# Casting the two halves of P around the relu in an attention and FFN kernel, with one VectorE order changed behind a hash

## The chip, the cores and the metric

The kernel runs on one core of a Trainium2 chip. The metric is the device time of one execution in microseconds; the kernel before took 977.11 us (median of three runs, 977.09 to 977.16).

A core has engines that work side by side, each through its own list of instructions in order: TensorE (PE; its weight loads are shown apart as PEld), VectorE (DVE), ScalarE (ACT), GpSimd (POOL) and SyncE (SP), which here issues nearly all DMAs.

## The reference

Attention with a hash mask over 32 heads (4 batches of 8, 768 tokens, 64 dimensions), and an FFN over its 3072 tokens:

```python
q_bits = (np.einsum('bhsd,dk->bhsk', q, proj) > 0).astype(np.int64)
k_bits = (np.einsum('bhsd,dk->bhsk', k, proj) > 0).astype(np.int64)
q_bucket = np.sum(q_bits * powers, axis=-1)
k_bucket = np.sum(k_bits * powers, axis=-1)
mask = q_bucket[:, :, :, None] == k_bucket[:, :, None, :]
scores = np.where(mask, scale * np.matmul(q, k.transpose(0, 1, 3, 2)), -1000000000.0)
attn = np.exp(scores - np.max(scores, axis=-1, keepdims=True))
attn = attn / (np.sum(attn, axis=-1, keepdims=True) + 1e-09)
x = np.matmul(attn, v)            # heads side by side: 3072 x 512
h = x @ w_in                      # 512 x 2048
g = h * np.clip(h + 3.0, 0.0, 6.0) / 6.0
return (g @ w_out).astype(np.float32)
```

## The kernel before, in words

Every operand of a large matmul is split into a high part, rounded to the PE's faster fp32 form, and a low part, the rest. So each product is made of two or three passes, and each operand costs a cast (ACT) and a subtraction (DVE or POOL).

The work is cut into steps k, one for each head and each block of 128 queries (32 heads x 6 blocks = 192 steps). From step 102 on (`GT`) the attention of batches 2 and 3 runs beside the FFN of batches already done; this is the function `beside_ffn`, and the change lies in it. The FFN takes 256 tokens at a time (a chunk) and 16 slices of its hidden dimension (`fc`), so one slice for each step, and a chunk for 16 steps. The order of each engine's instructions is the order in which the code issues them; only SP's order is chosen by a scheduler.

One step k from 102 on issues, in this order:

- PE, odd k only: `values_whole` (L512), a block of twelve matmuls that multiplies V with P of steps k-3 and k-2: three matmuls each for the high part of half 0, the high part of half 1, the low part of half 0, the low part of half 1. A half is 384 of the 768 keys.
- DVE: `lowest` (L396), called rounding in the change's title, reads the scores of step k+2 from PSUM, caps them and finds the lowest.
- ACT and DVE: the gate's split of the FFN slice of step k-1 (`split_g`): a cast to the high part (L681), and the low part (L682).
- ACT: the exponential of step k+2 (L408). DVE: its transposition in blocks of 32 (`flip`, L429). SP: the DMA that writes it to DRAM (`fd`), from where a later step's four DMAs read it back rearranged (`move`, into `px` or `spare` in turn). A buffer is free for the next `move` when the casts and subtractions of a step have read it.
- `split_p` of step k-1, for half 0 and half 1: two casts on ACT (L475, one row x2 in the timeline), then the subtraction of half 0 on DVE (L479) and of half 1 on POOL (L477).
- PE: the first product of the FFN slice (`gemm1`, L653). ACT: in even steps, a copy of the output of the last block of L512 (L542, `y<-acc`).
- PE, one step in six: the hash products of the next head (L334 to L336).
- PE: the second product of the slice before (`gemm2`, L691, L692 with the gate's high part, L696 with its low part). ACT: the relu (L675). DVE: the gate's product (L676). When the slice before was the last of its chunk, ACT also copies the FFN's result out of PSUM (L710, two instructions). This is in the part called `go("C")`.
- DVE, where there was a hash: its bits (L352). PE: the scores of step k+3 (L387, L389). At the end of a chunk the next tokens are split (casts on ACT, L642; low parts on DVE, L643).

The gate's high and low part have one buffer, so its cast waits for the second product of the slice before.

Of the kernel before, what the change touches and what calls it, by code (L numbers as in the profile page):

```python
# [28 lines left out]
LA = 3  # L29
# [3 lines left out]
LT = 1  # L33
# [10 lines left out]
def lsh_attention_moe(  # L44
# [10 lines left out]
    nc = tc.nc  # L55
# [3 lines left out]
    KT = S // P  # L59
    HW = S // 2  # L60
    QT = HW // P
# [31 lines left out]
    def bank(shape, name: str, tag: str | None = None):  # L93

        nonlocal turn
        if tag is None:
            tag = ("pt", "pu")[turn % 2]
            turn += 1
        return ps.tile(shape, F32, name=name, tag=tag, bufs=2)
# [128 lines left out]
    NS = NJ * KT  # L228
# [3 lines left out]
    GT = GF + FT  # L232
# [37 lines left out]
    def scale_q(i: int):  # L270

        for c in spans(i):
            if paced:
                nc.scalar.mul(raws[i][:D, c], raws[i][:D, c], -SCALE)
            else:
                nc.gpsimd.tensor_scalar_mul(raws[i][:D, c], raws[i][:D, c], -SCALE)
# [114 lines left out]
    def lowest(g: int):  # L391

        s = scs.pop(g)
        m = sp.tile([P, 1], F32, name=f"m{g}", tag="m", bufs=4)
        pr_ = sp.tile([P, 2, HW], F32, name=f"p{g}", tag="p", bufs=2)
        nc.vector.tensor_scalar(  # L396
            out=pr_[:], in0=s[:, :, :HW], scalar1=CAP, scalar2=None,
            op0=ALU.min, op1=ALU.min, accum_out=m[:],
        )
        probs[g] = pr_, m  # L400
# [82 lines left out]
    def split_lows():  # L483
        for f in lows:
            f()
        lows.clear()
# [18 lines left out]
    def values_whole(u: int):  # L505
        vv = vvs[2 * u // KT]
        acc = accs[u] = bank([P, 2 * P], f"acc{u}")
        both = [parts.pop((u, c)) for c in range(2)]
        for part in range(2):
            for kt in range(KT):  # L510
                c, x = divmod(kt, QT)
                nc.tensor.matmul(  # L512
                    acc[:], lhsT=vv[:, kt], rhs=both[c][part][:, x],
                    start=(part == 0 and kt == 0), stop=(part == 1 and kt == KT - 1),
                )

    adds = []

# [263 lines left out]
    def cv(n: int):  # L782

        if n < NW:
            if n not in conv:
                conv[n] = convert(n)
            next(conv[n])
# [299 lines left out]
    with tc.manual_schedule(engines={ET.PE, ET.DVE, ET.Activation, ET.Pool}):  # L1087
        split_qk(0, None)
        hash_qk(0)
        bits(0)  # L1090
        scale_q(1)
        split_v(0)
        for x in range(3):
            ahead(0, x)
        for _ in range(2):
            cv(0)
        def go(part: str):
            if stage == part:
                next(fill, None)

        through = []

        def beside_ffn(k: int):

            nonlocal paced, stage, held
            held = False
            if k < GT:
                for c in range(2):  # L1110
                    transp(k, c)
                exponential(k + 1)
            for _ in range(2):
                u = vnext // 2
                if u < NS // 2 and (2 * u < GT or k % 2 and k >= 2 * u + 3):
                    if vnext % 2 == 0 and k >= GT:
                        value_whole()
                        through.append(u)
                        break
                    if value_half():  # L1120
                        through.append(vnext // 2 - 1)
                if k < GT:
                    break
            if k == GT:
                opening.pop()()
            if k + 2 < NS and k >= GT:
                lowest(k + 2)
            go("A")
            if k < GT:
                for c in range(2):  # L1130
                    split_p(k, c, False)
                split_lows()
                while through:
                    output(through.pop(0))
                flip(k + 1)
            if k + 2 < NS:
                if k < GT:
                    lowest(k + 2)
                exponential(k + 2)
            paced = True  # L1140
            multiply()
            if k + 2 < NS:
                flip(k + 2)
            if GT <= k - LT < NS:
                for c in range(2):
                    split_p(k - LT, c, False)
            split_lows()
            go("B")
            if k == NS + LT:
                homes.clear()  # L1150
            while through and (through[0] < vnext // 2 - 1 or k % 2 == 0 or k < GT):
                output(through.pop(0))
            hashed = k + LA < NS and (k + LA) % KT == 4 and (k + LA) // KT + 1 < NJ
            if hashed:
                hash_qk((k + LA) // KT + 1)
            go("C")
            if hashed:
                bits((k + LA) // KT + 1)
            if k + LA < NS:
                lead(k + LA)  # L1160
            if moves:
                moves.pop(0)()
            if GT <= k + 1 < NS:
                move(k + 1)

            place_in_chunk = (k - GT) % NFC
            if subs and (k % 2 and (k < GT or place_in_chunk != NFC - 1) or k > GT and place_in_chunk == 0):
                subs.pop(0)()
            go("D")
            if k % KT in (1, 3):  # L1170
                add()

        for k in range(NS + LT + 2):
            if k >= GT - 1:
                beside_ffn(k)
                continue
            end = GB if k < GB else NS
            i, t = divmod(k, KT)
            if k == HK - XE:
                lent += lents[cc3:]  # L1180
            if k == GB:
                lent.clear()
            if k == HK:
                late["x"] = sp.tile([P, S], F32, name="late", tag="raw", bufs=1)
            for c in range(2):
                transp(k, c)
            if k + 1 < end:
                exponential(k + 1)
            if k + 2 < end:
                lowest(k + 2)  # L1190
            if k == GB:
                next(first)
                pair_turn = 0

            third = True
            whole = False
            for _ in range(1 if k != HK else 2):
                if vnext < k - k % 2:
                    whole = value_half()
            held = k >= GF - 2  # L1200
            if held:
                next(fill, None)
            if whole and k >= GF:
                output(vnext // 2 - 1)
                whole = False

            hashed = k >= GF and (k + LA) % KT == 2
            if k >= GF and k + LA < end and not hashed:
                lead(k + LA)
            for c in range(2):  # L1210
                split_p(k, c, third)
            split_lows()
            multiply()
            held = False
            if (k < GF or hashed) and k + LA < end:
                if hashed:
                    if (k + LA) // KT + 1 < NJ:
                        hash_qk((k + LA) // KT + 1)
                        bits((k + LA) // KT + 1)
                    next(fill, None)  # L1220
                lead(k + LA)
            if k == GB - 2:
                hash_qk((GB - 1) // KT + 1)
                bits((GB - 1) // KT + 1)
            if whole:
                output(vnext // 2 - 1)
            if k >= GF - 2 and not hashed:
                next(fill, None)
            if k < GB:
                for f in early_steps[k]:  # L1230
                    f()

            if k < HK and t == 1 and i:
                with tc.issue_after(last.ins):
                    load_w(i)
            if k == HK:
                add()
                late_x()
                with tc.issue_after(last.ins):
                    get_qk(H + 2)  # L1240
                    for n in range(WE, WL):
                        load_w(n)
            if k + 1 == GB:
                first = first_ffn(lambda part: ahead(GB, part))
                next(first)
                for _ in range(2):
                    whole = value_half()
                output(vnext // 2 - 1)
                next(first)
        paced = False  # L1250
        assert vnext == NS and not through
        add()
        for _ in fill:
            pass
# [47 lines left out]
```

## Time and profile before

| | |
|---|---|
| median of three runs | 977.11 us |
| profiled execution | 976.93 us |
| its span | 975.2 us |
| granted TensorE clock, mean | 0.997 |
| PE, PEld, DVE, ACT, POOL busy | 98%, 90%, 74%, 64%, 49% |
| matmuls of L512, steps beside the FFN | 552 |

The span is the time from the first to the last instruction that the profile shows. A row of the timeline has the start in us, the duration, the engine, the line, the operation, what it writes and reads, and how many instructions were merged; in brackets stands how long its engine was idle before it and what ended that. A row of the waits has the total in us, how often, and the longest. In the window's row PE, PEld, DVE, ACT and POOL follow each other, then the clock, the share of DMA and GB/s. Matmuls overlap, so a merged row of PE ends later than the next one begins.

### The profile page before, as it was taken

What the parts mean: (1) busy time and instruction counts of PE and PEld (TensorE: products, weight loads), DVE (VectorE), ACT (ScalarE), POOL (GpSimd) and SP (SyncE); (2) the same over time, 40 slices, a digit from 0 to 9 for tenths busy, and PEclk for the clock granted to TensorE, in tenths of its full rate; (3) what the DMA queues carried; (4) which work ended last, traced back from release to release, by engine and by line L of the source; (5) the groups of instructions that cost most, each with busy time, mean ns of one, the idle gap of its engine ahead of it and who ended that gap; (6) DMA issues with size and microseconds to landing.
All of it is one profiled execution on the core that took longest, in us unless ns stands there. A gap on an engine that the chain in (4) does not pass through costs nothing.

```text
span 975.2 us, 19413 instructions
## 1 busy us (share of the span) xinstructions
PE 951.2 (98%) x6306; PEld 875.4 (90%) x6306; DVE 716.8 (74%) x1476; ACT 626.9 (64%) x1421; POOL 480.8 (49%) x498
## 2 busy tenths in 40 slices
PE   8999999999999998899999999999999999999997
PEld 7999888999989998799999889999999899889896
DVE  7999988888569998777777778878777774342422
ACT  6898875656478887567766666676676664333332
POOL 6777744655537775355555546546556542000000
PEclk9999999999999999999999999999999999999999
DMA  3567579100035544688798787788787772101000
GB/s 118 139 163 179 133 237 374 42 2 1 6 118 126 124 111 123 181 249 237 227 258 243 230 245 235 234 264 243 237 266 229 218 225 69 44 1 44 1 22 22
DMA packets 113116, 151.65 MB, mean 156 GB/s; under 512 B 13764, under 2 KB 82116, under 8 KB 113016
## 3 DMA queue, kind: packets, MB, share of 16 engines
q1 hardware_dynamic: 108456, 144.79, 48.7%
q0 software_dynamic: 4560, 5.64, 4.8%
q8 instruction: 50, 0.82, 0.4%
q14 instruction: 50, 0.41, 0.1%
HBM read 77.34 MB, written 53.61 MB: 134 GB/s over the span
## 4 chain that ended last, share of the span: by engine, by line
PE 80%; DVE 9%; issue 3%; POOL 3%; DMA 2%; ACT 2%; SPq 1%; DVEq 0%; ACTq 0%; POOLq 0%
PE h L653 26%; PE po L696 6%; PE po L691 6%; PE po L692 6%; PE acc L500 6%; PE acc L512 6%; PE s L389 5%; PE s L387 5%; PE pt L418 5%; DVE p L396 3%; DVE pl L479 2%; POOL pl L477 2%; DVE qq L352 1%; PE z L334 1%; PE z L335 1%
## 5 line engine op out<-in xcount | busy, mean ns | idle before, releaser
L408 ACT ACTIVATE p<-p,m 128x768 f32<-128x768 f32 x192 | 180.2, 939 | 92.7 <-DVE p L396 87.9
L396 DVE TENSOR_SCALAR_CACHE_REDUCE p<-s 128x768 f32<-128x768 f32 x192 | 182.9, 953 | 40.4 <-PE s L389 24.9
L676 DVE SCALAR_TENSOR_TENSOR h<-g,h 128x256 f32<-128x256 f32 x192 | 81.9, 426 | 95.3 <-ACT g L675 93.4
L675 ACT ACTIVATE g<-h,three 128x256 f32<-128x256 f32 x192 | 91.0, 474 | 91.5 <-PE h L653 89.6
L653 PE MATMUL h<-xh,w 128*128 128x256 f32 x1024 | 147.0, 283 | 1.6 <-ACT xh L642 1.6
L653 PEld LDWEIGHTS h<-xh,w 128*128 128x128 f32 x1024 | 135.7, 189 | 5.1 <-ACT xh L642 1.8
L429 DVE STREAM_TRANSPOSE p<-p 128x768 f32<-128x768 f32 x90 | 88.1, 979 | 60.3 <-ACT p L408 60.3
L477 POOL TENSOR_TENSOR pl<-spare,ph 128x384 fp32r<-128x384 f32 x45 | 62.4, 1388 | 117.7 <-ACT ph L475 82.2
L479 DVE TENSOR_TENSOR pl<-pt,ph 128x384 fp32r<-128x384 f32 x196 | 100.0, 550 | 3.5 <-ACT ph L475 3.0
L681 ACT CAST gb<-h 128x256 fp32r<-128x256 f32 x141 | 52.5, 372 | 77.2 <-DVE h L676 44.0
L387 PE MATMUL s<-kk,qq 76*128 76x384 f32 x384 | 100.1, 341 | 1.8 <-ACT kk L357 1.5
L389 PE MATMUL s<-kk,qq 128*128 128x384 f32 x384 | 100.4, 343 | 0.0
L692 PE MATMUL po<-w,gb 128*128 128x512 f32 x250 | 98.3, 393 | 0.0
L691 PE MATMUL po<-w,gb 128*128 128x512 f32 x250 | 98.3, 393 | 0.0
L477 POOL TENSOR_TENSOR pl<-px,ph 128x384 fp32r<-128x384 f32 x45 | 61.6, 1370 | 72.6 <-ACT ph L475 58.5
L475 ACT CAST ph<-pt 128x384 fp32r<-128x384 f32 x196 | 86.0, 473 | 14.7 <-PE pt L418 12.7
L216 POOL TENSOR_TENSOR w<-wr,w 128x128 fp32r<-128x128 f32 x128 | 72.0, 594 | 45.2 <-ACT w L210 42.1
L418 PE MATMUL pt<-ident,p 128*128 128x128 f32 x612 | 85.9, 274 | 3.6 <-DVE pl L479 2.7
L418 PEld LDWEIGHTS pt<-ident,p 128*128 128x128 f32 x612 | 71.7, 141 | 11.1 <-PE pt L418 2.5
L653 PE MATMUL h<-xl,w 128*128 128x256 f32 x512 | 81.5, 281 | 0.0
L696 PE MATMUL po<-w,gb 128*128 128x512 f32 x250 | 78.8, 396 | 1.5 <-DVE gb L682 1.5
L387 PEld LDWEIGHTS s<-kk,qq 76*128 76x128 f32 x384 | 66.7, 190 | 11.3 <-ACT kk L357 2.1
(153 smaller groups left out, 2133.4 us busy)
## 6 DMA issues: line engine op xcount, KB each, us to landing
fd<-p SPq DMA_DIRECT2D x90, 384.0 KB
spare<-fd SPq DMA_DIRECT2D x180, 96.0 KB
px<-fd SPq DMA_DIRECT2D x180, 96.0 KB
kk<-qq SPq DMA_DIRECT2D x62, 192.0 KB
wr<-in_w_in SPq DMA_DIRECT2D x16, 512.0 KB
wr<-in_w_out SPq DMA_DIRECT2D x16, 512.0 KB
raw<-in_qkT SPq DMA_DIRECT2D x19, 384.0 KB
vr<-in_v SPq DMA_DIRECT2D x32, 192.0 KB
```

The source lines that it names most:

```text
L387: nc.tensor.matmul(s[:, c, :HW], lhsT=q1[:KM, us], rhs=half(k1[:KM], c), start=True, stop=False)
L389: nc.tensor.matmul(s[:, c, :HW], lhsT=q2[:, us], rhs=half(k2, c), start=False, stop=True)
L396: nc.vector.tensor_scalar(out=pr_[:], in0=s[:, :, :HW], scalar1=CAP, scalar2=None, op0=ALU.min, op1=ALU.min, accum_out=m[:],)
L408: nc.scalar.activation(pr_[:], pr_[:], AF.Exp, bias=m[:], scale=-1.0, accum_out=sms[b][:, t, h : h + 1])
L418: nc.tensor.transpose(pt[:, x], probs[g][0][:, c, x * P : (x + 1) * P], ident[:])
L477: engine.tensor_sub(lo, pt, hi.bitcast(F32))
L479: lows.append(lambda: engine.tensor_sub(lo, pt, hi.bitcast(F32)))
L653: nc.tensor.matmul(hp, lhsT=wi[:, wp, wc], rhs=x[cc][xp], start=(k == 0 and cc == 0), stop=(k == 2 and cc == NCC - 1),)
L675: nc.scalar.activation(r[:], hp, AF.Relu, bias=three[:], scale=1.0)
L691: nc.tensor.matmul(po[u], lhsT=gh[:, us], rhs=wo[:, 0], start=(fc == 0), stop=False)
L692: nc.tensor.matmul(po[u], lhsT=gh[:, us], rhs=wo[:, 1], start=False, stop=False)
L696: nc.tensor.matmul(po[u], lhsT=gl[:, us], rhs=wo[:, 0], start=False, stop=(fc == NFC - 1))
```

## The change

In `beside_ffn`, for the steps from 102 on, half 1 of P (POOL's) is cast first, and half 0 (DVE's) only behind `go("C")`, that is, behind the relu; its subtraction stands behind the gate's product on DVE. `values_whole` takes half 1 ahead of half 0. In the step behind one with a hash, the gate's low part comes ahead of `lowest` on DVE.

```diff
         both = [parts.pop((u, c)) for c in range(2)]
+        first, end = (0, 1, 0), (1, 0, QT - 1)
         for part in range(2):
-            for kt in range(KT):
-                c, x = divmod(kt, QT)
-                nc.tensor.matmul(
-                    acc[:], lhsT=vv[:, kt], rhs=both[c][part][:, x],
-                    start=(part == 0 and kt == 0), stop=(part == 1 and kt == KT - 1),
-                )
+            for c in (1, 0):
+                for x in range(QT):
+                    nc.tensor.matmul(
+                        acc[:], lhsT=vv[:, c * QT + x], rhs=both[c][part][:, x],
+                        start=(part, c, x) == first, stop=(part, c, x) == end,
+                    )
...
-            if k + 2 < NS and k >= GT:
+            behind = (k - 1 + LA) % KT == 4
+            if GT <= k < NS - 2 and not behind:
                 lowest(k + 2)
             go("A")
+            if GT <= k < NS - 2 and behind:
+                lowest(k + 2)
...
-            if GT <= k - LT < NS:
-                for c in range(2):
-                    split_p(k - LT, c, False)
-            split_lows()
+            split = GT <= k - LT < NS
+            if split:
+                split_p(k - LT, 1, False)
             go("B")
...
             go("C")
+            if split:
+                split_p(k - LT, 0, False)
+            split_lows()
```

On ACT at step 118, where a chunk of the FFN ends (`ph` are the casts of P, `y` the copy of a block's output, `g` the relu, `ob` the copies of the FFN's result, `gb` the gate's cast), the rows before:

```order
L408 ACTIVATE p_6545,sms_5284<-p_6545,m_6544 128x768
L475 CAST ph_0_6490<-px 128x3x128
L475 CAST ph_1_6493<-px 128x3x128
L542 COPY y_0_6571<-acc_6466 128x256
L675 ACTIVATE g_1_0_6580<-h_1_0_6558,three 128x256
L710 ACTIVATE ob_0_6583<-po_0_5595 128x512 x2
L681 CAST gb_1_0_6614<-h_1_0_6558 128x256
```

And now, at the same place (line numbers have moved by one):

```order
L408 ACTIVATE p_6545,sms_5284<-p_6545,m_6544 128x768
L475 CAST ph_1_6490<-px 128x3x128
L543 COPY y_0_6569<-acc_6466 128x256
L676 ACTIVATE g_1_0_6578<-h_1_0_6556,three 128x256
L711 ACTIVATE ob_0_6581<-po_0_5595 128x512 x2
L475 CAST ph_0_6516<-px 128x3x128
L682 CAST gb_1_0_6614<-h_1_0_6556 128x256
```

The cast of half 0 has moved behind the y copy, the relu and both copies of the FFN's result; in a step inside a chunk the rows are the same without the `ob` row.

On DVE at steps 133 and 134, where a hash, the end of a chunk and the step behind the hash come together (`pl` is the low part of P's half 0, `h` the gate's product, `qq` the hash bits, `xl` the next tokens' low parts, `gb` the gate's low part, `m` marks `lowest`), the rows before:

```order
L429 STREAM_TRANSPOSE p_7470<-p_7470 128x768
L479 TENSOR_TENSOR pl_0_7481<-spare,ph_0_7480 128x3x128
L676 SCALAR_TENSOR_TENSOR h_1_15_7488<-g_1_15_7515,h_1_15_7488 128x256
L352 TENSOR_SCALAR qq_7261<-z_0_7501,thr,val 44x384
L352 TENSOR_SCALAR qq_7261<-z_1_7502,thr,val 44x384
L643 TENSOR_TENSOR xl_2_7534<-xr_2_7132,xh_2_7533 128x256 x4
L396 TENSOR_SCALAR p_7545,m_7544<-s_7524 128x768
L682 TENSOR_TENSOR gb_1_15_7547<-h_1_15_7488,gb_1_15_7547 128x256
```

And now:

```order
L429 STREAM_TRANSPOSE p_7470<-p_7470 128x768
L677 SCALAR_TENSOR_TENSOR h_1_15_7484<-g_1_15_7511,h_1_15_7484 128x256
L479 TENSOR_TENSOR pl_0_7515<-spare,ph_0_7514 128x3x128
L352 TENSOR_SCALAR qq_7261<-z_0_7497,thr,val 44x384
L352 TENSOR_SCALAR qq_7261<-z_1_7498,thr,val 44x384
L644 TENSOR_TENSOR xl_2_7534<-xr_2_7128,xh_2_7533 128x256 x4
L683 TENSOR_TENSOR gb_1_15_7544<-h_1_15_7484,gb_1_15_7544 128x256
L396 TENSOR_SCALAR p_7548,m_7547<-s_7524 128x768
```

The low part of P's half 0 has moved behind the gate's product, and the gate's low part ahead of `lowest`.

On PE the block of L512 (here of step 109) keeps its place; its halves have changed theirs. Before:

```order
L389 MATMUL s_5943<-kk_5455,qq_5456 128x384 x2
L512 MATMUL acc_5953<-ph_0_5862,vv_5662 128x256 x3
L512 MATMUL acc_5953<-ph_1_5865,vv_5662 128x256 x3
L512 MATMUL acc_5953<-pl_0_5863,vv_5662 128x256 x3
L512 MATMUL acc_5953<-pl_1_5866,vv_5662 128x256 x3
```

And now:

```order
L389 MATMUL s_5943<-kk_5455,qq_5456 128x384 x2
L513 MATMUL acc_5953<-ph_1_5862,vv_5662 128x256 x3
L513 MATMUL acc_5953<-ph_0_5888,vv_5662 128x256 x3
L513 MATMUL acc_5953<-pl_1_5863,vv_5662 128x256 x3
L513 MATMUL acc_5953<-pl_0_5889,vv_5662 128x256 x3
```

The block now begins with POOL's half, and the high part of DVE's half is read from the fourth matmul on, the low part of POOL's half from the seventh.

## The prediction

> **What bounds the kernel now.** I read the page first, then the waits and the windows of the stage that the change touches, then the chain of waits and the timeline of single steps.
>
> ```profile
> span 975.2 us, 19413 instructions
> PE 951.2 (98%) x6306; PEld 875.4 (90%) x6306; DVE 716.8 (74%) x1476; ACT 626.9 (64%) x1421; POOL 480.8 (49%) x498
> ```
> ```profile
> 396.00:820.00 424.00, 418.03 (x2698) 384.68 (x2696) 321.41 (x635) 279.55 (x653) 223.86 (x195) 1.00 0.79 234
> ```
> ```profile
> PEld acc L512 <- POOL pl L477: 5.1, 12, 0.5
> PEld po L696 <- DVE gb L682: 3.2, 4, 1.4
> PE acc L512 <- POOL pl L477: 2.7, 11, 0.3
> ```
> PE bounds the kernel. In the stage of the change (396 to 820 us: steps 102 to 190) it is idle for 424.00 - 418.03 = 6.0 us, at full clock, with DMA at 0.79. What ends last there is the low part of P that POOL makes (L477), ahead of the matmuls at L512. The chain of waits shows what a block of twelve such matmuls takes:
> ```profile
> 423.98 1.57 PE acc L512 x12
> ...
> 432.56 1.59 PE acc L512 x12
> ...
> 459.86 1.42 PE acc L512 x12
> ...
> 800.78 1.57 PE acc L512 x12
> ```
> Of the stage's 45 blocks 19 look like the first, second and fourth row; the third has other PE work ahead of it and waits for nothing. A regular block thus loses 1.57 - 1.42 = 0.15 us. One of them in full (step 108, and the block of step 109):
> ```profile
> 431.03 0.91 ACT L475 CAST ph<-px 128x384 fp32r<-128x384 f32 x2
> 431.85 0.36 ACT L542 COPY y<-acc 128x256 f32<-128x256 f32 x1
> 432.11 0.47 ACT L675 ACTIVATE g<-h,three 128x256 f32<-128x256 f32 x1
> ```
> ```profile
> 431.16 0.98 DVE L429 STREAM_TRANSPOSE p<-p 128x768 f32<-128x768 f32 x1 [0.76 <-ACT p L408]
> 432.06 0.52 DVE L479 TENSOR_TENSOR pl<-px,ph 128x384 fp32r<-128x384 f32 x1
> 432.62 0.43 DVE L676 SCALAR_TENSOR_TENSOR h<-g,h 128x256 f32<-128x256 f32 x1
> ```
> ```profile
> 432.07 1.39 POOL L477 TENSOR_TENSOR pl<-px,ph 128x384 fp32r<-128x384 f32 x1 [1.42 <-DMA spare<-fd]
> ```
> ```profile
> 432.22 0.84 PEld L512 LDWEIGHTS acc<-ph,vv 128*128 128x128 f32 x6
> 433.00 0.94 PEld L512 LDWEIGHTS acc<-pl,vv 128*128 128x128 f32 x6
> 433.87 0.43 PEld L653 LDWEIGHTS h<-xh,w 128*128 128x128 f32 x3
> ```
> The wait sits on the weight load. Loads follow each other by about 0.12 us, so the tenth (first of POOL's half) is due at 433.00 + 3 x 0.12 = 433.36; POOL ends at 433.46, a signal takes 0.05 (POOL's end at 478.54 + 1.41 = 479.95 and the load at 480.00, both below), and 0.15 are lost.
>
> **The change, part by part: regular blocks.** POOL's cast goes first: two casts take 0.91, the second begins 0.41 behind the first, so POOL can start at about 431.60 instead of 432.07. How long its subtraction takes then is shown by a step where DVE's came early:
> ```profile
> 565.50 0.56 DVE L479 TENSOR_TENSOR pl<-spare,ph 128x384 fp32r<-128x384 f32 x1 [0.27 <-ACT ph L475]
> ...
> 565.90 1.02 POOL L477 TENSOR_TENSOR pl<-spare,ph 128x384 fp32r<-128x384 f32 x1 [3.20 <-ACT ph L475]
> ```
> 1.02 alone against 1.39 beside DVE's. With 1.02 it ends at 432.62, with 1.39 at 432.99; its matmuls are now the seventh to ninth, whose first load is due at 433.00, so it must end by 432.95. I take 1.02, since DVE's subtraction now comes after it: spare 0.33. At 1.39 it would miss by 0.04. The Trainium skill ("SBUF — State Buffer", Who interferes with whom) says the same of the cause: a VectorE instruction with two SBUF inputs and a GpSimd instruction that reads SBUF share a port pair, and the later one blocks wholly; by that rule 1.02 holds wherever POOL is first. The two rows agree with the price, but at 432.06 both start together and POOL alone pays, so the order of the records does not tell who gets it.
>
> DVE's half goes later. The y copy follows the one remaining cast at 431.44, the relu 0.26 later at 431.70, and what follows a relu starts 0.37 behind it (478.62 to 478.99, below), so the cast of DVE's half runs from 432.07 to 432.57. Its matmuls are now the fourth to sixth, whose first load is due half way from 432.22 to 433.00, the span of the first six loads: at 432.61. With the signal's 0.05 it comes at 432.62, just in time. DVE's subtraction then ends at 433.12, due at 433.31. I take no wait: 19 x -0.15 = -2.85 us; bounds 0 (a cast 0.15 late) and -2.85.
>
> **Chunk ends.** Every 16 steps ACT also copies the FFN's result out (L710, 10 instructions in the stage, so five steps: 118, 134, 150, 166, 182). Step 118 and the block of step 119:
> ```profile
> 477.54 0.91 ACT L475 CAST ph<-px 128x384 fp32r<-128x384 f32 x2
> 478.35 0.37 ACT L542 COPY y<-acc 128x256 f32<-128x256 f32 x1
> 478.62 0.48 ACT L675 ACTIVATE g<-h,three 128x256 f32<-128x256 f32 x1
> 478.99 1.08 ACT L710 ACTIVATE ob<-po 128x512 f32<-128x512 f32 x2
> 479.94 0.39 ACT L681 CAST gb<-h 128x256 fp32r<-128x256 f32 x1
> ```
> ```profile
> 478.32 0.84 PEld L512 LDWEIGHTS acc<-ph,vv 128*128 128x128 f32 x6
> 479.13 0.41 PEld L512 LDWEIGHTS acc<-pl,vv 128*128 128x128 f32 x3
> 480.00 0.41 PEld L512 LDWEIGHTS acc<-pl,vv 128*128 128x128 f32 x3 [0.46 <-POOL pl L477]
> 480.35 1.01 PEld L653 LDWEIGHTS h<-xh,w 128*128 128x128 f32 x8
> ```
> ```profile
> 478.54 1.41 POOL L477 TENSOR_TENSOR pl<-px,ph 128x384 fp32r<-128x384 f32 x1 [3.65 <-ACT ph L475]
> ```
> Today both casts stand ahead of the two copies and the block loses 480.35 - 478.32 - 1.42 - 0.06 = 0.55 (0.06: loads from the block's first to the next line's span 433.87 - 432.22 = 1.65 in the regular block, which counts 1.59). Afterwards the cast of DVE's half stands behind them: one cast less ahead, so relu at 478.21, copies at 478.58 and 479.06, cast from 479.53 to 480.04. Its load is due half way from 478.32 to 479.13, at 478.73, and comes at 480.09: 1.36 late, 0.81 worse than today. Lower bound: +0.3, if such a step starts no later than a regular one; upper: +1.3.
>
> **Behind a hash** (every sixth step) the gate's low part (L682) goes ahead of the rounding (L396). Mostly the scores that the rounding waits for come after it: 0.03 lost. Not where DVE is late already, at steps 134 and 182 (a chunk end too) and 128 and 176:
> ```profile
> 547.79 1.92 DVE L643 TENSOR_TENSOR xl<-xr,xh 128x256 fp32r<-128x256 f32 x4
> 549.74 0.96 DVE L396 TENSOR_SCALAR_CACHE_REDUCE p<-s 128x768 f32<-128x768 f32 x1
> 550.63 0.08 DVE L396 DVE_READ_ACCUMULATOR p<-s 128x1 f32 x1
> 550.63 0.42 DVE L682 TENSOR_TENSOR gb<-h,gb 128x256 fp32r<-128x256 f32 x1
> ```
> ```profile
> 551.10 0.30 PEld L696 LDWEIGHTS po<-w,gb 128*128 128x128 f32 x2 [0.46 <-DVE gb L682]
> ```
> There the rounding starts 0.34 later (0.42 less the overlap of 0.08) and with it the exponential, the casts and the block. PE's wait for the low part at 551.10 goes, but the block behind it takes that back, since it waits for ACT anyway. So 0.81 + 0.34 = 1.15 at 134 and 182. At 128 and 176 the lateness grows by 0.34 and by about 0.25 that DVE loses when its subtraction, now behind the gate, waits for POOL: 0.6 each.
>
> The sum: regular -2.85; chunk ends 3 x 0.81 + 2 x 1.15 = +4.7; 128 and 176 +1.2; of the other irregular blocks seven have casts that are late for other reasons, and there the cast that now comes 0.63 later (432.07 against 431.44) costs between -0.15 and +0.4, taken as +0.2: +1.4. Together +4.5 on the profiled execution's 976.93 (span 975.2 and 1.7 around it; the median of the runs is 977.11, 0.2 more): 981.5. Other moves cost nothing: POOL, SP and PE keep their instructions, and bits and x's splits on DVE still end before the next scores.
>
> **Rivals.** *The regular cast misses too* (chance 0.20, slower): it has nothing to spare. A y copy or relu that starts 0.15 later undoes the gain of all 19: 981.5 + 2.85 = 984.4. Against it: the ACT rows are the same within 0.02 in the regular blocks.
>
> *Transfers come earlier* (0.18, no change): POOL's input buffer is free when the later subtraction ends, at 433.12 instead of 433.46, and the move into it can go 0.34 earlier. Where a step waits for transfers today,
> ```profile
> 568.28 0.96 DVE L396 TENSOR_SCALAR_CACHE_REDUCE p<-s 128x768 f32<-128x768 f32 x1 [1.63 <-PE h L653]
> ```
> ```profile
> 569.64 0.30 PEld L696 LDWEIGHTS po<-w,gb 128*128 128x128 f32 x2 [0.88 <-DVE gb L682]
> ```
> (the 1.63 of idle time end with a DMA; the PE work named was long done) PE loses 0.88 and, in the block behind it, as much as in another late one, 0.55: 1.4. Two more places wait for casts whose input lands late; at half of that each the whole is 2.8, and the time 981.5 - 2.8 = 978.7. Against it: after a chunk end the buffer is free later.
>
> *DVE catches up* (0.12, faster): the first of the four splits at 547.79 takes 0.9 instead of 0.4 behind a POOL instruction; POOL now ends 0.8 earlier in each step. If each late step caught up 0.9, chunk ends would cost 5 x (1.36 - 0.90 - 0.55) = -0.4, steps 128 and 176 nothing, the seven -1.0, and the whole -4.3: 972.7. It decides from 0.8 of relief per chunk end; the rows show 0.5.
>
> **The numbers.** The main case has 0.50. A measurement of this kernel can tell 0.2% (2 us) from no change. Faster 0.12, the same 0.18, slower 0.70. The range reaches from 978.0, below the case of transfers, to 985.5, above that of the missed cast; the faster case and the tails are left out.
>
> **What would show it.** Right: blocks of 1.42 after regular steps; POOL's subtraction at about 1.0; the load of the fourth matmul after a chunk end waiting for ACT's cast by over 1 us, five times. Wrong: regular blocks that wait for ACT's cast (the first rival), or chunk-end blocks near 2.0 us as today.

## The result, and the profile after

The changed kernel takes 986.75 us (median of four runs, 985.31 to 989.38), the kernel before 977.13 beside it (four runs, 977.09 to 977.99): a ratio of 1.0099, interval 1.0076 to 1.0123. It is slower, as forecast, but by 9.6 us where 4.4 were forecast, and above the range. The profiled execution took 985.31, 8.4 more than the 976.93 of before.

The head of the page after:

```profile
span 983.5 us, 19374 instructions
PE 952.3 (97%) x6306; PEld 875.9 (89%) x6306; DVE 727.8 (74%) x1476; ACT 626.9 (64%) x1421; POOL 456.3 (46%) x498
```

POOL works 24.5 us less and DVE 11 more. The same stretch of the stage, and two short stretches in it (the last three numbers of a row are the granted clock, the share of DMA and GB/s):

```profile
396.00:820.00 424.00, 410.87 (x2644) 378.27 (x2643) 328.24 (x625) 276.13 (x644) 198.14 (x194) 0.99 0.80 233
...
480.00:485.00 5.00, 3.99 (x21) 3.79 (x22) 3.56 (x5) 2.23 (x6) 2.11 (x2) 0.73 0.65 226
485.00:490.00 5.00, 5.00 (x29) 4.51 (x28) 3.36 (x6) 2.55 (x6) 2.24 (x2) 0.93 0.79 238
```

PE is idle for 13.1 us of the stretch instead of 6.0, and at one place its clock is low, which it never was in the stage before after 410 us. What PE waits for at the block of twelve matmuls, now L513, in the waits of the stage:

```profile
PEld acc L513 <- ACT ph L475: 11.2, 14, 1.5
PE acc L513 <- ACT ph L475: 9.4, 13, 1.3
...
PEld acc L513 <- DVE pl L479: 1.9, 3, 0.6
```

POOL's low part is gone from the list. In its place stand the cast of half 0 (ACT), and, three times, the low part of half 0 (DVE).

A regular block came out as forecast. The step 108 and the block of step 109 in the timeline after, all engines in one list:

```profile
431.50 0.50 ACT L475 CAST ph<-px 128x384 fp32r<-128x384 f32 x1
...
432.12 1.02 POOL L477 TENSOR_TENSOR pl<-px,ph 128x384 fp32r<-128x384 f32 x1 [1.37 <-ACT ph L475]
...
432.53 0.51 ACT L475 CAST ph<-px 128x384 fp32r<-128x384 f32 x1
...
432.68 0.84 PEld L513 LDWEIGHTS acc<-ph,vv 128*128 128x128 f32 x6
...
433.07 0.56 DVE L479 TENSOR_TENSOR pl<-px,ph 128x384 fp32r<-128x384 f32 x1
...
433.45 0.79 PEld L513 LDWEIGHTS acc<-pl,vv 128*128 128x128 f32 x6
```

POOL's subtraction takes 1.02 instead of 1.39, the second cast comes 1.03 behind the first and is just in time, and the loads show no wait. The chain of waits has the block of this step, and that of the regular step before it, at the length of a block without a wait:

```profile
424.59 1.43 PE acc L513 x12
433.02 1.43 PE acc L513 x12
```

The end of a chunk did not. Step 118 and the block of step 119 in the timeline after:

```profile
478.60 1.01 POOL L477 TENSOR_TENSOR pl<-px,ph 128x384 fp32r<-128x384 f32 x1 [4.26 <-DMA spare<-fd]
478.68 0.48 ACT L676 ACTIVATE g<-h,three 128x256 f32<-128x256 f32 x1
478.77 0.49 PEld L513 LDWEIGHTS acc<-ph,vv 128*128 128x128 f32 x3
...
479.05 1.08 ACT L711 ACTIVATE ob<-po 128x512 f32<-128x512 f32 x2
...
479.69 1.82 POOL L318 TENSOR_TENSOR kk<-raw,qq 64x768 fp32r<-64x768 f32 x1
480.00 0.53 ACT L475 CAST ph<-px 128x384 fp32r<-128x384 f32 x1
...
480.56 1.37 DVE L479 TENSOR_TENSOR pl<-px,ph 128x384 fp32r<-128x384 f32 x1 [0.94 <-DMA kk<-qq]
480.58 0.41 PEld L513 LDWEIGHTS acc<-ph,vv 128*128 128x128 f32 x3 [1.32 <-ACT ph L475]
...
481.98 0.43 PEld L513 LDWEIGHTS acc<-pl,vv 128*128 128x128 f32 x3 [0.63 <-DVE pl L479]
...
482.33 0.73 PEld L654 LDWEIGHTS h<-xh,w 128*128 128x128 f32 x3
```

By the prediction's measure (first load of the block to the first load of the next line, less 1.48) the block loses 482.33 - 478.77 - 1.48 = 2.08 us, 0.55 before. Two waits make it up: for the cast, which the prediction has, and for DVE's subtraction, which it has not. That one takes 1.37 instead of 0.55, because it meets L318, in which POOL splits a head's keys for the hash.

Where the next tokens' high parts stand behind the moved cast, the first product of the new chunk is late too; its load at step 118, after (before, 0.36 behind the line ahead of it as everywhere, with no wait):

```profile
474.09 0.37 PEld L389 LDWEIGHTS s<-kk,qq 128*128 128x128 f32 x2
474.75 1.57 PEld L654 LDWEIGHTS h<-xh,w 128*128 128x128 f32 x8 [0.29 <-ACT xh L643]
```

### The profile page after: what moved, and what is told of

It is laid out like the page before. It is cut to its first block, busy times and chain, and to the rows that moved or that the text cites. A ratio compares the mean times of both kernels' runs of the same rounds, so it can differ in the third digit from the quotient of the medians.

```text
span 983.5 us, 19374 instructions
## 1 busy us (share of the span) xinstructions
PE 952.3 (97%) x6306; PEld 875.9 (89%) x6306; DVE 727.8 (74%) x1476; ACT 626.9 (64%) x1421; POOL 456.3 (46%) x498
## 4 chain that ended last, share of the span: by engine, by line
PE 77%; DVE 9%; ACT 4%; DMA 3%; issue 3%; SPq 1%; POOL 1%; ACTq 0%; DVEq 0%; POOLq 0%
PE h L654 25%; PE po L697 6%; PE po L692 6%; PE po L693 6%; PE acc L500 6%; PE acc L513 5%; PE pt L418 5%; PE s L389 5%; PE s L387 5%; DVE p L396 3%; DVE pl L479 3%; ACT ph L475 2%; DVE qq L352 1%; SPq L78 1%; DMA spare<-fd 1%
## 5 line engine op out<-in xcount | busy, mean ns | idle before, releaser
L477 POOL TENSOR_TENSOR pl<-spare,ph 128x384 fp32r<-128x384 f32 x45 | 45.7, 1016 | 140.0 <-ACT ph L475 79.6
L475 ACT CAST ph<-pt 128x384 fp32r<-128x384 f32 x196 | 86.1, 473 | 15.1 <-PE pt L418 13.1
L477 POOL TENSOR_TENSOR pl<-px,ph 128x384 fp32r<-128x384 f32 x45 | 46.1, 1024 | 73.7 <-ACT ph L475 50.2
```

The costliest lines, as they stand in the source:

```text
L475: nc.scalar.copy(hi, pt)
L477: engine.tensor_sub(lo, pt, hi.bitcast(F32))
```

## The experiments

The theory behind the first of them: the loss comes from the five chunk ends, where the cast of half 0 stands behind the two copies of the FFN's result; what goes beyond the forecast there is DVE's subtraction beside POOL's L318, and a lower clock behind long waits. The rivals: the loss is spread over the steps (the exchange behind a hash, or transfers), or the order of the casts itself is wrong. The times of a run stand beside runs of the kernel before on the same chip, 976.66 to 977.06 by the median.

**The cast ahead of the copies.** In the changed kernel the cast and the subtraction of half 0 are issued ahead of the copies where a chunk ends; everywhere else they stay. (The FFN's code empties the list below just ahead of its copies.)

```diff
             if split:
-                split_p(k - LT, 0, False)
-            split_lows()
+                ahead_of_copies.append(lambda: late_half(k - LT))
+            go("C")
+            while ahead_of_copies:
+                ahead_of_copies.pop(0)()
```

> The changed kernel, with one thing different: at the five chunk ends the cast of DVE's half stands behind the relu but ahead of the two copies of the FFN's result (0.96 us of ACT). Theory (chunk ends: the cast waits behind the copies, then DVE's subtraction behind a POOL instruction, then a lower granted clock): the wait for the cast falls from 1.28 to 1.60 us to 0.3 to 0.6 at each of the five, the 0.68 behind the low part goes at three of them or stays, no stretch at a clock of 0.7; 978 to 981 us. Rival (DVE's two new orders are what costs: the subtraction behind the gate's product, the gate's low part ahead of the rounding): within 1.5 us of the changed kernel's 986.8.

It took 978.02 us (976.37 to 980.04, ten runs), a ratio of 1.0011 (0.9998 to 1.0023) to before: 8.7 of the 9.6 us are gone, with everything else of the change in place. The block of step 119 in its timeline:

```profile
479.89 0.48 PEld L513 LDWEIGHTS acc<-ph,vv 128*128 128x128 f32 x3
...
480.71 0.56 DVE L479 TENSOR_TENSOR pl<-px,ph 128x384 fp32r<-128x384 f32 x1
480.73 0.41 PEld L513 LDWEIGHTS acc<-ph,vv 128*128 128x128 f32 x3 [0.36 <-ACT ph L475]
...
480.82 2.17 POOL L318 TENSOR_TENSOR kk<-raw,qq 64x768 fp32r<-64x768 f32 x1
481.08 0.79 PEld L513 LDWEIGHTS acc<-pl,vv 128*128 128x128 f32 x6
```

The wait for the cast falls from 1.32 to 0.36, and the one for the low part is gone: DVE's subtraction now starts 0.11 ahead of L318, takes 0.56, and L318 pays (2.17 instead of 1.82). In the stretches from 410 us on no clock is below 0.98. So the chunk ends hold the loss; which of the three parts has how much is for the next two runs.

**POOL's subtraction of the keys one step later.** In the changed kernel, at two of the five chunk ends (steps 118 and 166), L318 moves to the step behind.

```diff
+            hold = k > GT and place_in_chunk == 0 and k % KT == 4
-            if subs and (k % 2 and (k < GT or place_in_chunk != NFC - 1) or k > GT and place_in_chunk == 0):
+            if subs and (k % 2 and (k < GT or place_in_chunk != NFC - 1) or k > GT and place_in_chunk == 0 and not hold):
+                subs.pop(0)()
+            if subs and k > GT and place_in_chunk == 1 and k % KT == 5:
                 subs.pop(0)()
```

> The changed kernel with POOL's 1.82 us subtraction of a head's keys moved one step on, at two of the five chunk ends (steps 118 and 166). Theory (VectorE's subtraction takes 1.37 instead of 0.55 us there only because POOL's subtraction of the keys runs beside it): the waits of 0.69 us for the low part go at blocks 119 and 167 and stay at 151, the time is 984 to 985.5 (986.75 less 1.36, and less up to 1.5 where the low clock behind block 119 goes too), unless the two subtractions that POOL then has in the step behind make a wait of their own. Rival (the low part is late by its place in VectorE's order, whatever POOL does): the waits of 0.69 stay and the time is 986.75.

It took 985.04 us (983.41 to 986.51, five runs). In its timeline DVE's subtraction at step 118, and then the step behind with the two moved subtractions:

```profile
480.57 0.56 DVE L479 TENSOR_TENSOR pl<-px,ph 128x384 fp32r<-128x384 f32 x1 [0.94 <-DMA kk<-qq]
...
484.64 2.03 POOL L318 TENSOR_TENSOR kk<-raw,qq 64x768 fp32r<-64x768 f32 x1
...
486.75 1.84 POOL L318 TENSOR_TENSOR qq<-raw,qq 64x768 fp32r<-64x768 f32 x1
...
488.67 1.01 POOL L477 TENSOR_TENSOR pl<-px,ph 128x384 fp32r<-128x384 f32 x1
...
488.97 1.13 DVE L479 TENSOR_TENSOR pl<-px,ph 128x384 fp32r<-128x384 f32 x1
...
489.74 0.83 PEld L513 LDWEIGHTS acc<-pl,vv 128*128 128x128 f32 x6 [0.31 <-POOL pl L477]
```

At the same start and place as in the changed kernel (480.57 against 480.56) DVE's subtraction takes 0.56 instead of 1.37, and block 119 has no wait for it. The waits for DVE's low part in the stage fall from three to one, the one at step 151. The rival, that it is late by its place, falls. The block itself loses 0.84 more than before (1.39 against 0.55), where the prediction had 0.81. Little of it stays gained: POOL is then late in the step behind, where the block waits 0.31 for it and DVE's subtraction takes 1.13. The Trainium skill ("SBUF — State Buffer", Who interferes with whom) says that of a VectorE instruction with two SBUF inputs and a GpSimd instruction that reads SBUF the later one blocks for all of the other. The traces agree: in the changed kernel L318 ends at 479.69 + 1.82 = 481.51 and DVE's subtraction at 480.56 + 1.37 = 481.93, 0.42 behind it.

The low clock has moved with it. The stretches of this run at block 119 and at block 135:

```profile
480.00:485.00 5.00, 4.41 (x30) 4.16 (x31) 3.65 (x7) 3.33 (x9) 1.37 (x2) 1.00 0.77 261
555.00:560.00 5.00, 4.01 (x21) 4.01 (x22) 2.78 (x6) 3.35 (x8) 1.02 (x2) 0.68 0.83 275
```

Block 119 now loses about 1.4 and keeps its clock; block 135, the first to lose over 2 us, has the drop.

**PE kept busy in the wait.** In the changed kernel, twelve matmuls whose result is overwritten stand ahead of the block behind each chunk end.

```diff
+        for _ in range(4 if 2 * u + 3 > GT + 1 and (2 * u + 3 - GT) % NFC == 1 else 0):
+            for x in range(QT):
+                nc.tensor.matmul(
+                    acc[:], lhsT=vv[:, QT + x], rhs=both[1][0][:, x], start=True, stop=True
+                )
```

> The changed kernel with twelve more matmuls (1.4 us) at the start of the block behind each chunk end; their result is overwritten, and they stand where PE waits for ACT's cast. Theory (the granted clock falls because PE stands still for over 1 us twice within 3 us, and this is why the runs of the changed kernel spread from 985.3 to 989.4): no stretch below a clock of 0.95 behind a chunk end, and 983 to 985 us in every run. Rival (the clock has nothing to do with the waits): a stretch near 0.7 as before, 985 to 989 us.

It took 984.89 us (983.37 to 987.67, four runs). The stretch at block 119:

```profile
480.00:485.00 5.00, 4.61 (x35) 4.19 (x34) 3.71 (x6) 2.94 (x8) 2.11 (x2) 1.00 0.79 260
```

The full clock held in the whole stage beyond 410 us. At block 119 nothing else has changed: the next line's first load stands at 482.32, against 482.33 in the changed kernel. So it is the idle time of PE ahead of it that the drop goes with; this is one execution. The changed kernel lost 5.00 x (1 - 0.73) + 5.00 x (1 - 0.93) = 1.7 us by it. From the copies of step 118 to those of step 134 this run takes 554.70 - 479.02 = 75.68, the changed kernel 556.12 - 479.05 = 77.07: 1.4 less. That the medians give 986.75 - 984.89 = 1.9 is partly chance, since the two profiled executions as a whole differ by only 0.1 (985.31 and 985.18). The second half of the expectation failed: one run still took 987.67, at a mean clock of 0.997, so something else spreads the runs too. In the changed kernel the clock has a part in it: the run of 989.38 had a mean clock of 0.990 and the profiled one 0.993, which is some (0.993 - 0.990) x 983.5 = 3.0 of the 4.1 us between them. The rest stays open.

**Without the exchange behind a hash**, and then **the exchange alone** on the kernel before.

```diff
-            behind = (k - 1 + LA) % KT == 4
+            behind = False
```

> The changed kernel without the swap behind a hash: the rounding ahead of the gate's low part in every step, as before. Theory: the swap costs 0.34 us at steps 128, 134, 176 and 182 and about 0.08 in each of ten regular blocks behind a hash, and saves a wait for the gate's low part of 0.4 at one or two places: 984.5 to 986.5 us. Rival (the swap is the main loss): below 981.

The changed kernel without the exchange took 982.43 us (980.38 to 983.39, five runs), 2 us below what I expected. Before with the exchange and nothing else:

> The kernel before with one edit of the change alone: behind a hash the gate's low part comes ahead of the rounding. Theory (the exchange costs by itself what it cost in the changed kernel, 986.75 - 982.43 = 4.3 by the medians and 410.62 - 408.49 = 2.1 us by the stage of the two profiled runs): 979 to 981.5. Rival (its price arises only where the cast of the DVE half stands behind the relu, since a later rounding is then late for that cast; alone it costs nothing): 976.5 to 977.6. What I wrote in the prediction for it, 0.34 at two places and 0.6 at two, is about 2: 979.

It took 978.63 us (976.78 to 982.72, twelve runs), a ratio of 1.0024 (1.0013 to 1.0035): 2.0 us by the medians. The waits of its stage show one that the kernel before has not:

```profile
PEld acc L512 <- POOL pl L477: 6.2, 16, 0.5
...
PE acc L512 <- ACT ph L475: 1.6, 4, 0.6
```

Four blocks wait for ACT's casts, and POOL's wait comes on top. The rounding ahead of them starts 0.34 behind the gate's low part, which has its old place (746.02 against 745.68 at step 176), on a DVE that is late already; that this is the cause is argued from the rows and not tried by itself. So the exchange costs 2 us by itself, in agreement with the sum of the prediction, 0.34 x 2 + 0.6 x 2 = 1.9; the rival that it is free alone falls. Why it costs 4.3 by the medians in the changed kernel, and only 985.31 - 982.43 = 2.9 by the profiled executions, these runs don't tell.

**Half 1 cast and used first, and nothing else.** The kernel before with `split_p` called for half 1 and then half 0, both ahead of the relu as before, and `values_whole` in that order.

```diff
             if GT <= k - LT < NS:
-                for c in range(2):
+                for c in (1, 0):
                     split_p(k - LT, c, False)
             split_lows()
```

> Before, with POOL's half of P cast first and used first, and nothing else: both casts stay ahead of the relu, DVE's subtraction ahead of the gate's product, no swap behind a hash. Theory: POOL's subtraction starts 0.41 earlier and takes 1.0 instead of 1.4 because DVE's now comes after it; the 19 regular blocks gain 0.15 each, chunk ends lose nothing and gain up to 0.4: 972.5 to 975 us. Rival (DVE's subtraction is held back by POOL's and with it the gate's product and the next rounding): 977 us or more.

It took 986.62 us (984.53 to 987.68, four runs): the theory fell and the rival held. In the groups of the stage, DVE's subtraction in this kernel and in the kernel before:

```profile
L479 DVE TENSOR_TENSOR pl<-px,ph 128x384 fp32r<-128x384 f32 x45 | 46.9, 1042 | 1.0 <-ACT ph L475 0.8
```
```profile
L479 DVE TENSOR_TENSOR pl<-px,ph 128x384 fp32r<-128x384 f32 x45 | 23.4, 520 | 0.4 <-ACT ph L475 0.4
```

1.04 instead of 0.52: now POOL is first and DVE pays, and everything behind it on DVE is later. That POOL needs 0.37 less buys nothing, since DVE loses 0.52. Most of the loss comes where the later DVE meets POOL once more: 1.75 + 1.88 + 1.77 = 5.4 of the 7.6 us between the profiled executions (984.53 and 976.93) arise just ahead of and in blocks 113, 145 and 161, by the starts of the blocks' last loads. In the steps ahead of them a small DVE instruction, which adds 1e-9 to the sums of the exponentials (128x16, L561, L560 before), now runs into L318 and takes 1.77, 1.47 and 1.77; before it took some 0.65.

**Both casts ahead of the relu, DVE's subtraction behind the gate.** If the harm is DVE's subtraction beside POOL's, and the late cast, then both should go at once.

```diff
             if split:
                 split_p(k - LT, 1, False)
+                split_p(k - LT, 0, False)
             go("B")
...
             go("C")
-            if split:
-                split_p(k - LT, 0, False)
             split_lows()
```

> The changed kernel with both casts ahead of the relu, POOL's half first, VectorE's subtraction behind the gate's product as in the change, and without the exchange behind a hash. Theory (the gain comes from keeping VectorE's subtraction out of POOL's way and the loss from the cast that stands behind the relu and the copies; the relu was never what set the end): regular blocks without a wait, POOL's subtraction 1.02 us, no wait for the cast at the chunk ends: 971 to 974.5. Rival (the relu is 0.4 us later than in the change, so the gate's product, VectorE's subtraction behind it and the next rounding come late, as the POOL half first did by itself at 986.62): 977 or more.

It took 992.49 us (991.46 to 994.3, five runs), the slowest of all; the theory fell. A regular step in its timeline:

```profile
433.32 0.47 ACT L676 ACTIVATE g<-h,three 128x256 f32<-128x256 f32 x1
433.43 0.84 PEld L513 LDWEIGHTS acc<-ph,vv 128*128 128x128 f32 x6
...
433.82 0.43 DVE L677 SCALAR_TENSOR_TENSOR h<-g,h 128x256 f32<-128x256 f32 x1 [0.48 <-ACT g L676]
...
434.16 0.55 DVE L479 TENSOR_TENSOR pl<-px,ph 128x384 fp32r<-128x384 f32 x1
434.20 0.98 PEld L513 LDWEIGHTS acc<-pl,vv 128*128 128x128 f32 x6
```

DVE is idle 0.48 for the relu, and its subtraction, queued behind the gate's product, ends at 434.71. The six loads take 0.98 where they took 0.79 in the changed kernel: 0.2 lost in a regular block. At the chunk ends with an L318 the subtraction meets it and takes 1.99, and the load waits 1.90. By these rows the relu between the casts is no by-product: it lets the gate's product start early enough that DVE's subtraction can stand behind it. I had taken the relu for free, as something that never set the end.

**The cast ahead of the copies and no exchange.** The first run's edit with `behind = False`.

> The changed kernel with the cast and the subtraction of the DVE half ahead of the FFN's output copies at a chunk's end, and without the exchange behind a hash. Theory (the two costs add: copies ahead of the cast 986.75 - 978.02 = 8.7, the exchange 2.1 to 4.3): 973.7 to 976, faster than the kernel before. Rival (the exchange costs only by way of the chunk ends, where the later rounding moves the late cast, so with the cast ahead of the copies it is free): 977.5 to 978.5.

It took 975.88 us (973.51 to 978.12, twelve runs), 0.9991 of before (0.9981 to 1.0), and 2.1 below the first run, so the exchange costs about the same 2 us here, and the rival falls.

**The output copy behind the cast.** In that kernel, the copy of the attention output (L543) is moved from ahead of the relu to behind the cast of half 0 and the FFN's copies.

```diff
             go("B")
             if k == NS + LT:
                 homes.clear()
-            while through and (through[0] < vnext // 2 - 1 or k % 2 == 0 or k < GT):
-                output(through.pop(0))
...
             while ahead_of_copies:
                 ahead_of_copies.pop(0)()
+            while through and (through[0] < vnext // 2 - 1 or k % 2 == 0 or k < GT):
+                output(through.pop(0))
```

> The kernel of the run at 975.88 (cast ahead of the FFN's output copies, no exchange behind a hash) with the copy of the attention output moved from ahead of the relu to behind the cast of the DVE half. Theory (a block waits for that cast by its place in ScalarE's order, and the copy of 0.36 us, 0.26 from its start to the relu's, is the last thing ahead of it that can go): the waits of 0.42 at blocks 119 and 167 and of about 0.6 at 135, 151 and 183 fall by 0.26 each, those behind a hash (0.24 at 129 and 177) go, together 1.3 to 1.8 us: 974 to 975. Rival (the copy then frees its bank or sends its rows later, or the wait is set by the relu's own start and not by the order): 975.5 to 976.5.

It took 974.49 us (973.44 to 976.95, twelve runs), a ratio of 0.9977 (0.9964 to 0.999): faster than the kernel before by 0.2%, and the best of these kernels. ACT at step 118 and the block behind it in its timeline:

```profile
477.21 0.49 ACT L475 CAST ph<-px 128x384 fp32r<-128x384 f32 x1
...
477.62 0.46 ACT L676 ACTIVATE g<-h,three 128x256 f32<-128x256 f32 x1
...
477.98 0.50 ACT L475 CAST ph<-px 128x384 fp32r<-128x384 f32 x1
477.99 0.96 PEld L513 LDWEIGHTS acc<-ph,vv 128*128 128x128 f32 x6
...
478.39 1.08 ACT L711 ACTIVATE ob<-po 128x512 f32<-128x512 f32 x2
```

Casts and relu now follow each other with nothing between, and the block's first six loads take 0.96 where a regular block's take 0.84: some 0.1 of a wait is left of the 0.37 that the run before has there.

## Why the prediction was right and wrong

*Regular blocks*: right in mechanism, somewhat too high in size. The subtraction of 1.02, the cast that is just in time, and blocks of 1.43 are as worked out. By the start of each block's last load, ten of the 19 gain 0.14 to 0.18. The five behind a hash (111, 123, 141, 159, 171) gain only 0.06 to 0.08, since the fourth load waits there some 0.1 for the cast, and block 153 loses 0.13. With 155 at +0.07 (0.99 later, of which 0.92 come back by 157) and 121, where the clock is low, taken at -0.15, the 19 come to some -1.9 instead of -2.85. So the rival that the regular cast misses happened in a small part.

*Chunk ends, the wait for the cast*: right in place and size, 1.36 forecast and 1.32 measured. All five waited over 1 us for it.

*Chunk ends, the whole term*: wrong, and the main miss. I had 3 x 0.81 + 2 x 1.15 = 4.7. Blocks 119 and 167 lose 2.08 instead of 0.55 (+1.53 each), 151 2.25 instead of 0.69 (+1.56). At 135 and 183 it is 2.20 instead of 0.80 (+1.40 each), and some 0.16 each come back, since the wait for the gate's low part ahead of them goes (0.46) while the low parts of the new chunk's tokens come later: together 7.1. These two, +1.24 each, are near the 1.15; the miss is at the other three. The prediction follows a late cast to the load that needs it and stops there; it takes DVE's subtraction at 0.55 wherever it lands. Where it landed, at 480.56, POOL was in L318: 0.7 more at 119, 151 and 167. At 135 and 183, with no L318 at that time, the subtraction took 0.56. This is shown by the run with L318 a step later.

*Left out*: the clock, 1.7 us, put at nothing although the trace of before has such a drop at the start of the stage (half the clock from 403.15 to 406.56, behind a wait of 1.6); and the first products of new chunks, 0.3 each at 118 and 166. I wrote that other moves cost nothing, but on ACT the next tokens' casts stand behind the moved one. So 7.1 + 1.7 + 0.6 = 9.4 stand at the chunk ends against the profiled 8.4, and the rest of the change comes to about -1.0, where the prediction had -2.85 + 1.2 + 1.4 = -0.25. That the whole is not further off is partly luck: with -1.9 for the regular blocks, the irregular ones cost only some 0.9, where 2.6 were forecast.

*Behind a hash*: the size of 1.9 was right for the exchange alone (2.0), but not place by place: alone, by the last loads, it costs 0.31 at block 129, 0.72 at 135, 0.72 at 177 and 0.33 at 183. In the changed kernel the 0.6 at 128 and 176 was too much: their blocks wait 0.3 longer with the exchange than without it (0.52 against 0.21 ahead of the fourth load at block 129), which is the 0.34 of the later rounding; the 0.25 for a DVE held by POOL did not come.

*Irregular blocks and transfers*: some went (the block of step 139 lost 0.28 instead of 0.80), others came (0.9 ahead of the fourth load at 145, where POOL's half cost 0.49 before, and a wait of 1.02 for the gate's low part at 144). What came is the main miss once more, at another DVE instruction. The rows of step 144 after:

```profile
597.32 2.03 POOL L318 TENSOR_TENSOR qq<-raw,qq 64x768 fp32r<-64x768 f32 x1
...
597.58 1.80 DVE L561 TENSOR_SCALAR rc<-sms 128x16 f32<-128x16 f32 x1
```

Before, this instruction took 0.65 and L318 started only 0.05 behind its end. Now it stands behind the late subtraction, starts inside L318 and ends 0.03 behind it (599.38 and 599.35); the rounding and the gate's low part behind it are late, and both waits follow. By the start of the last load, block 145 comes 1.33 later for it. It takes 1.80 with the cast ahead of the copies and 1.81 in the last run too, so this cost is still in the fastest kernel; no run moved it by itself. Nor did a run try the transfers by themselves. The median is 1.4 above the profiled execution; in part this is the clock (above), and the rest stays open.

## What to carry to other kernels

When an instruction is moved later, follow it past the first wait that it makes: ask what its own successors then meet, and, between DVE and POOL above all, which instruction of the other engine is running at that moment. A transposition of order that helps the regular step must be worked out for the irregular one (here one step in sixteen), and the repair may be one instruction there: the same change with the cast ahead of the copies, without the exchange and with the output's copy behind the cast is faster than the kernel before (0.9977 of its time). And parts of one change can hold each other up: half 1 first alone, or with the casts both ahead of the relu, cost 10 to 16 us.

## What the runs showed of the hardware

The granted clock fell behind waits of PE that are short by themselves: in the changed kernel behind 1.32 and 0.63 us, which end 1.4 us apart (0.73 over the next stretch of 5 us). It fell once each from 410 us on in the four profiled kernels in which a block lost over 2 us with nothing to fill it (0.73, 0.66, 0.68, 0.72 in the lowest stretch). The seven profiled kernels without such a block, or with the waits filled, had none. In finer windows the drop behind block 119 looks like this:

```profile
478.92:482.33 3.41, 1.87 (x14) 1.46 (x13) 2.39 (x4) 1.89 (x5) 2.51 (x2) 1.00 0.94 344
482.33:485.74 3.41, 3.41 (x17) 3.31 (x16) 1.79 (x4) 1.80 (x4) 1.26 (x2) 0.50 0.39 99
```

PE stood still for 3.41 - 1.87 = 1.54 us of the first window and had half the clock in all of the second. All these drops last 3.41 us, and the one at the start of this stage, at 403.83, begins 78.50 us = 23 x 3.413 earlier. So the clock seems to be set in fixed windows of this length; that they count from the idle time in the window before is argued and not shown. Not each block of over 2 us is followed by a drop: the four other chunk ends of the changed kernel (135, 151, 167, 183) kept the clock. How much idle time in one window is enough stays open: 3.41 - 2.24 = 1.17 us ahead of the drop at 403.15 in the kernel before were, 3.42 - 1.95 = 1.47 at block 135 of the changed kernel (554.00 to 557.42) were not. The Trainium skill ("TensorE: Matmul & The Clock Gate", HAM oscillation — how this bites in real kernels) gives as the rule to leave no idle gap of PE above some 3.4 us; here gaps of less than half of that, one behind the other, were enough, and the measurement decides.

Where instructions of DVE and POOL run beside each other, one can keep its time while the other waits, in either direction: POOL's subtraction took 1.39 instead of 1.02 beside DVE's, DVE's 1.04 instead of 0.52 beside POOL's and 1.37 to 1.99 behind the start of L318, and L318 2.17 instead of 1.82 behind DVE's. The loser ended 0.42 behind L318 with 1.37 (481.93 and 481.51) as with 1.99 (483.61 and 483.19). Where the records start almost together their order does not tell who loses: at 478.54 and 478.56 in the kernel before POOL's starts first, and POOL's takes 1.41.
